# Values in front of a later duo's scores, in a bank of the first products, from block 1 on

## The chip, the cores and the metric

One core of a Trainium2 chip runs the whole program. The metric is the device time of one execution in microseconds (us). Below, PE is TensorE, PEld its weight loads, DVE VectorE, ACT ScalarE, POOL GpSimd and SP SyncE, whose queue issues the DMAs.

## The reference

```python
# q, k, v: (4, 8, 768, 64); mem_k, mem_v: 8 keys per head
for c in range(768 // 32):                      # chunks of 32 queries
    k_full = concat([mem_k, k[from 16 before the chunk to 8 behind it]])
    v_full = the same of mem_v, v
    s = q_c @ k_full.T / sqrt(64)
    a = exp(s - s.max(-1));  a = a / (a.sum(-1) + 1e-9)
    out[chunk] = a @ v_full
x = out, heads side by side                     # (3072, 512)
h = x @ w_in;  g = h * cos(h);  x = g @ w_out   # 512 -> 2048 -> 512
h = max(x @ w1, x @ w2, x @ w3);  x = h @ w_out2  # 512 -> 768 -> 512
```

The output is the last x, transposed, in fp32.

## The kernel before, in words

Each fp32 factor of the large products is split into a high and a low part, and a product is made as three passes over the parts (`PASSES`, `products`, L385 to L392). The program has two stages. The second, quads of the max of three products and the last product (`quad`, `pair_out`, lines L734 and L861), is not touched.

**The first stage** goes over `NBLK` = 6 blocks of 512 tokens, and within each over `FA` = 16 slots, one for each 128 of the 2048 columns of w_in. A slot (`slot`, from L980) issues:

- `p1`, the first products: 12 matmuls of 128x512 (L392, `h<-x,w`) into one bank, from the pool `ps_h` of two banks. The two banks are used in turn.
- `chain`: ACT rounds h (L450), DVE reduces it (L452, L453), ACT takes the sine (L455), DVE multiplies h with the cosine (L457), ACT takes the high part (L461) and POOL the low part (L462) of g. L457 is the last reader of the bank of h.
- `p2`, the second products of the slot two before (`LOOK` = 2): 12 matmuls (L392, `acc<-g`) into four accumulators. At a block's end they are copied out by ACT and DVE (L482, L484).

**Attention** for the following block is spread over these slots. A duo is 128 queries, four duos (`DB`) make a block, 24 (`ND`) the whole. The tables `FIRST` (block 0), `SECOND` (block 1) and `STEADY` (blocks 2 on) say what a slot does beside its products; a digit is a duo, counted from the next block's first, so 4 to 7 are duos of the block after next:

- S, scores: 32 small matmuls (L246) into two banks of the pool `ps_a`, two mask additions on DVE (L263), maximum and its subtraction (L269, L270), and the loads of q and k of two duos on.
- E, the exponentials of two duos on ACT (L274), with a table load ahead and another before the next sine.
- N, normalisation: sums (L279) and small operations on DVE, the product on POOL. T: a transpose on DVE and its store to DRAM. L or l: the load of the transposed weights `pt`.
- V, values: 32 small matmuls (L305) into a bank of `ps_a`, read by ACT (L307, the copy) and DVE (L308, the subtraction), which write the two parts of the next block's x.

What a slot's table names after T comes in the table's order. Before an S or a V the slot's second products were issued (`do2`), so PE ran first products, second products, attention. In block 4 nothing with a digit of 4 or more is left to do, and it is passed over. Preparation of the second stage's weights (L181, L198, L552, L553) runs on ACT, DVE and POOL beside the slots from slot 27 on. The orders of PE and SP are fixed as written from slot 6 on; ACT, DVE and POOL are ordered by the framework's scheduler, with parts of the chain held in line by `row`.

Of the kernel before, what the change touches and what calls it, by code (L numbers as in the profile page):

```python
# [9 lines left out]
F32 = mybir.dt.float32  # L10
# [13 lines left out]
S = 768  # L24
# [11 lines left out]
DB = N // (2 * QU)  # L36
# [11 lines left out]


FIRST = {2: "S0", 3: "S1", 4: "S2", 5: "S3 E01", 6: "E23 N0", 7: "T0 N1", 8: "L0 T1 N2", 9: "V0 l1", 10: "V1 T2 N3", 11: "L2 T3", 12: "V2 l3", 14: "V3"}  # L50
SECOND = {0: "S0", 1: "S1", 2: "E01 S2", 3: "N0 S3", 4: "T0", 5: "E23 N1 L0 S4", 6: "V0 T1", 7: "L1 N2", 8: "S5 T2 N3", 9: "V1 E45", 10: "L2 S6 T3", 11: "V2", 12: "L3 S7", 13: "V3", 14: "E67"}
STEADY = {1: "N0", 2: "T0 N1", 3: "L0", 4: "S4", 5: "V0 T1 N2", 6: "L1", 7: "S5", 8: "V1 T2 N3", 9: "L2 E45", 10: "S6 T3", 11: "V2 l3", 12: "S7", 13: "V3", 14: "E67"}

# [22 lines left out]
def attn_moe_kernel(ctx, tc, qT, kT, vw, w_in, w_out, w3, w2o, out):  # L78
# [23 lines left out]
    ps_h = ctx.enter_context(tc.tile_pool(name="ps_h", bufs=2, space=PSUM))  # L102
    ps_a = ctx.enter_context(tc.tile_pool(name="ps_a", bufs=2, space=PSUM))
# [145 lines left out]
    def a_scores(d):  # L249
        ss[d] = [ps_a.tile([128, 4, KU], F32, tag="a", name="s") for _ in range(2)]  # L250
        for t in range(2):
            a_s(d, t, ss[d][t], True, keep)
# [4 lines left out]
    def a_add(d):  # L257
        m = sm[d] = t2.tile([128, KB * H * 32], F32, tag="sm", name="sm", bufs=4)
        m = by_key(d)
        p = ss.pop(d)  # L260
        for t in range(2):
            mask = maskb[:, variant(d, t), None, :].to_broadcast([128, 4, KU])
            DVE.tensor_tensor(m[:, 4 * t:4 * t + 4], p[t].rearrange("p h (b k) -> p h b k", b=KB),  # L263
                              mask.rearrange("p h (b k) -> p h b k", b=KB), op=ALU.add)
# [7 lines left out]
    def a_exp(j, ds):  # L272
        for d in (DB * j + i for i in ds):
            keep(ACT.activation(out=sm[d], in_=sm[d], func=AF.Exp, scale=0.125))  # L274
# [14 lines left out]
    def a_l(d):  # L289
        pt[d] = t2.tile([128, 4, H, 32], F32, tag="pt", name="pt", bufs=1)  # L290
        for b in range(KB):
            keep(SP.dma_start(out=pt[d][32 * b:32 * b + 32].rearrange("p a h q -> p a (h q)"),
                              in_=ptd[d % 2][:, 256 * b:256 * b + 256].rearrange("(a p) e -> p a e", a=4)))

    def a_v(d):
        p, v = pt[d], vt[d]
        j, o = divmod(d, DB)
        if o == 0:
            xT[j] = xp.tile([128, 2, 4, N], F32R, tag="x", name="x")
        x = xT[j][:, :, :, 128 * o:128 * o + 128]  # L300
        s = ps_a.tile([128, 4, 128], F32, tag="a", name="s")
        for t in range(2):
            for h in range(H):
                p0 = 64 * (h % 2)
                keep(PE.matmul(s[p0:p0 + 64, h // 2, QU * t:QU * t + QU], lhsT=v[:KU, t, 64 * h:64 * h + 64],  # L305
                               rhs=p[:KU, 2 * (h % 2):2 * (h % 2) + 2, 4 * t + h // 2, :], start=True, stop=True))
        ACT.activation(out=x[:, 0], in_=s, func=AF.Copy)  # L307
        DVE.tensor_tensor(x[:, 1], s, x[:, 0].bitcast(F32), op=ALU.subtract)  # L308
# [85 lines left out]
    def p1(j, f):  # L394
        if f % 2 and (done[0] or j == 0 and f == 1):
            h = ps_a.tile([128, N], F32, tag="a", name="h")
        else:
            h = ps_h.tile([128, N], F32, tag="h", name="h")
        w, x = wA_in[f], xT[j]
        for k in range(4):  # L400
            products(h, w, k, [x[:, i, k, :] for i in range(2)], k == 0, k == 3)
        live[0] -= j == NBLK - 1
        hq[j, f] = h
# [4 lines left out]
    def wa_fetch(j, f):  # L408
        if j and f >= RES:
            w = w_tile([128, 2, 512], "wa")  # L410
            SP.dma_start(out=w.rearrange("p a c -> p (a c)").bitcast(F32), in_=wad[f])
            wA_out[f] = (w[:, 0, :], w[:, 1, :])
# [53 lines left out]
    def p2(j, f):  # L466
        g, w = g_t.pop((j, f)), wA_out[f]
        if f == 0:
            acc[j] = [ps_acc.tile([128, N], F32, tag=f"acc{m}", name=f"acc{m}") for m in range(4)]
        for m in range(4):  # L470
            products(acc[j][m], w, m, [g[:, i, :] for i in range(2 if j or f >= PLAIN else 1)], f == 0, f == FA - 1)
        live[0] -= f >= RES or j == NBLK - 1
        if f == FA - 1:
            for m in range(4):
                if m < 3:
                    t = tr.tile([128, N], F32, tag="r", name="x2")
                elif done[0]:
                    t = tmp["pool"].tile([128, N], F32, tag="xo", name="x2", bufs=6)
                else:
                    t = t2.tile([128, N], F32, tag="x2", name="x2", bufs=1)  # L480
                if m % 2 == 0:
                    ACT.activation(out=t, in_=acc[j][m], func=AF.Copy, scale=1.0 if j else -2.0)  # L482
                elif j:
                    DVE.tensor_copy(t, acc[j][m])  # L484
                else:
                    DVE.tensor_scalar(t, acc[j][m], -2.0, None, op0=ALU.mult)
                SP.dma_start(out=x2d[j][:, m, :], in_=t)
# [57 lines left out]
    def flush():  # L545
        while later:
            out, in_ = later.pop(0)
            keep(SP.dma_start(out=out, in_=in_))
# [61 lines left out]
    def prep_go(upto):  # L610
        while prep_n[0] < min(upto, len(prep)):
            prep[prep_n[0]]()
            prep_n[0] += 1
# [366 lines left out]
    def slot(s):  # L980
        j, f = slots[s]
        plan = {0: FIRST, 1: SECOND}.get(j, STEADY)
        todo = plan.get(f, "").split() if j < NBLK - 1 else []
        base = DB * (j + 1)

        ready = dec.nb
        if s < turn:
            dec.begin(RATE)
        if s < FA:
            parts = int(max(0, s - SPLIT0 + 1) * SPLITS[0])  # L990
        else:
            parts = int((FA - SPLIT0) * SPLITS[0] + (s - FA + 1) * SPLITS[1])

        def fill(where):
            if s < 2:
                if where == "z":
                    dec.split_in(ready)
                    dec.bits()
                    dec.load()
                return  # L1000
            if where == "z":
                prep_go(int(sum(i % FA not in QUIET for i in range(PREP0, s)) * PREPS))
            if s >= turn:
                if where == "z":
                    for fn in early.get(s - total, ()):
                        fn()
                return
            if where == "a0":
                dec.split_in(ready)
            elif where == "a1":  # L1010
                dec.split_out(parts)
            elif where == "d0":
                dec.bits(1)
            elif where == "z":
                dec.bits()
                dec.exp(dec.nb + 2)
                dec.load()

        for op in todo:
            if op[0] == "L" and base + int(op[1:]) < ND:  # L1020
                a_l(base + int(op[1:]))
        while wf[0] < min(s + (3 if s >= turn else 2), total):
            wa_fetch(*slots[wf[0]])
            wf[0] += 1
        flush()
        p1(j, f)
        chain(j, f, fill, [base + int(op[1:]) for op in todo if op[0] == "T" and base + int(op[1:]) < ND])

        def do2():
            while n2[0] <= s - LOOK:  # L1030
                p2(*slots[n2[0]])
                n2[0] += 1

        for op in todo:
            d = base + int(op[1:2])
            if d >= ND:
                continue
            if op[0] == "S":
                do2()
                a_scores(d)  # L1040
                a_add(d)
                a_load_qk(d + 2)
                a_max(d)
            elif op[0] == "E":
                a_exp(j + 1, map(int, op[1:]))
            elif op[0] == "N":
                a_norm(d)
            elif op[0] == "l":
                a_l(d)
            elif op[0] == "V":  # L1050
                do2()
                a_v(d)
                a_load_v(d + 2)
        do2()
# [32 lines left out]
    for p in range(NP):  # L1087
# [16 lines left out]
        todo = [["s11"], ["s1"], ["s3"], ["s21"], ["s2", "d4"], ["s22"], ["s4"]] if p + 1 < NP else []  # L1104
# [67 lines left out]
```

## Time and profile before

| | |
|---|---|
| median of three runs | 967.79 us (967.32 to 967.80) |
| profiled execution | 966.72 us |
| its span | 964.6 us |
| PE busy | 955.1 us, 99% of the span |
| DVE, ACT, POOL busy | 616.5, 461.4 and 410.3 us |

The profile shows one execution. The span runs from the first to the last recorded work; the execution's own time is 2.1 us longer. A busy engine's share is over both stages.

### The profile page before, as it was taken

How to read it: one execution, taken by the hardware profiler on the slowest of the kernel's cores; microseconds unless marked ns; L12 is line 12 of the kernel's file. 1: busy time of each engine (PE TensorE's matmuls, PEld its weight loads, DVE VectorE, ACT ScalarE, POOL GpSimd, SP SyncE). 2: the span in 40 equal slices, each digit the busy share in tenths (PEclk: the TensorE clock that was granted, in tenths of full speed). 3: DMA queues.
4: the chain of work that ended last, by engine and by line, in shares of the span. 5: the costliest groups of instructions: out<-in, count | busy, mean ns of one | idle time of the engine just before them, and what ended most of it. 6: DMA issues, size and time to landing. Idle time of an engine off the chain costs nothing.

```text
span 964.6 us, 14585 instructions
## 1 busy us (share of the span) xinstructions
PE 955.1 (99%) x5372; PEld 770.3 (80%) x5373; DVE 616.5 (64%) x926; ACT 461.4 (48%) x802; POOL 410.3 (43%) x329
## 2 busy tenths in 40 slices
PE   8999999999999999999999999999999999999998
PEld 5666888888888888888888888888888888888886
DVE  7688856655667666665655475644784657945565
ACT  6667745555445554564544545523363332723333
POOL 3566535534345445445433355435511545025520
PEclk9999999999999999999999999999999999999999
DMA  9986633563556855675476739694569647595502
GB/s 291 341 300 198 224 128 105 162 197 141 188 198 227 245 196 181 211 237 181 152 243 226 235 113 325 225 319 164 175 229 325 247 137 227 200 390 174 198 22 88
DMA packets 75911, 201.75 MB, mean 209 GB/s; under 512 B 8256, under 2 KB 21056, under 8 KB 75840
## 3 DMA queue, kind: packets, MB, share of 16 engines
q1 hardware_dynamic: 75552, 200.56, 61.9%
q8 instruction: 43, 0.70, 0.3%
q10 hardware_dynamic: 288, 0.26, 0.1%
q14 instruction: 28, 0.23, 0.1%
HBM read 154.13 MB, written 46.66 MB: 208 GB/s over the span
## 4 chain that ended last, share of the span: by engine, by line
PE 94%; DVE 3%; ACT 1%; issue 1%; DMA 1%; POOL 0%; SPq 0%; DVEq 0%; ACTq 0%
PE hb L734 27%; PE h L392 26%; PE acc L392 23%; PE hb L861 9%; PE s L246 3%; PE acc L389 3%; PE s L305 2%; PE warm L375 1%; DMA pt<-ptd 1%; PE s L356 0%; ACT ki L455 0%; DVE ki L453 0%; DVE ki L452 0%; DVE ki L457 0%; DVE mx L322 0%
## 5 line engine op out<-in xcount | busy, mean ns | idle before, releaser
L392 PE MATMUL h<-x,w 128*128 128x512 f32 x1152 | 283.8, 396 | 0.0
L392 PEld LDWEIGHTS h<-x,w 128*128 128x128 f32 x1152 | 213.2, 188 | 48.6 <-issue 1.4
L462 POOL TENSOR_TENSOR g<-ki,g 128x512 fp32r<-128x512 f32 x80 | 108.6, 1357 | 213.0 <-ACT g L461 186.9
L734 PE MATMUL hb<-x,wq 128*128 128x512 f32 x648 | 155.7, 389 | 0.0
L734 PEld LDWEIGHTS hb<-x,wq 128*128 128x128 f32 x648 | 121.6, 188 | 25.2
L392 PE MATMUL acc<-g,w 128*128 128x512 f32 x576 | 138.3, 389 | 0.0
L392 PEld LDWEIGHTS acc<-g,w 128*128 128x128 f32 x576 | 108.2, 188 | 22.4
L734 PE MATMUL hb<-xo,wq 128*128 128x512 f32 x486 | 119.1, 389 | 0.0
L392 PE MATMUL acc<-g,wa 128*128 128x512 f32 x480 | 115.6, 389 | 0.2 <-POOL g L462 0.2
L455 ACT ACTIVATE ki<-ki,pio 128x512 f32<-128x512 f32 x80 | 57.9, 723 | 109.3 <-DVE ki L453 109.3
L734 PEld LDWEIGHTS hb<-xo,wq 128*128 128x128 f32 x486 | 91.2, 188 | 18.9
L392 PEld LDWEIGHTS acc<-g,wa 128*128 128x128 f32 x480 | 90.0, 188 | 19.3 <-POOL g L462 0.6
L760 POOL TENSOR_TENSOR p<-p,p 128x512 f32<-128x512 f32 x27 | 38.3, 1420 | 144.9 <-ACT p L757 144.9
L452 DVE SCALAR_TENSOR_TENSOR ki<-h,ki 128x512 f32<-128x512 f32 x80 | 54.9, 687 | 69.3 <-ACT ki L450 69.3
L457 DVE TENSOR_TENSOR ki<-h,ki 128x512 f32<-128x512 f32 x80 | 55.2, 690 | 54.9 <-ACT ki L455 54.9
L861 PE MATMUL hb<-g,wo 128*128 128x512 f32 x378 | 86.2, 389 | 0.0
L861 PEld LDWEIGHTS hb<-g,wo 128*128 128x128 f32 x378 | 71.0, 188 | 14.7
L461 ACT ACTIVATE g<-ki 128x512 fp32r<-128x512 f32 x80 | 50.5, 631 | 59.3 <-DVE ki L457 59.1
L450 ACT ACTIVATE ki<-h 128x512 int32<-128x512 f32 x80 | 47.2, 590 | 60.0 <-PE h L392 53.5
L760 DVE TENSOR_TENSOR a<-a,hb 128x512 f32<-128x512 f32 x27 | 18.5, 684 | 72.1 <-PE hb L734 72.1
L553 DVE TENSOR_TENSOR wq<-raw,wq 128x512 fp32r<-128x512 f32 x36 | 44.1, 1243 | 25.0 <-ACT wq L552 25.0
L198 DVE SCALAR_TENSOR_TENSOR raw<-raw,top 128x512 int32<-128x512 int32 x48 | 46.1, 960 | 13.1 <-ACT top L181 11.7
(127 smaller groups left out, 1212.3 us busy)
## 6 DMA issues: line engine op xcount, KB each, us to landing
wq<-wd SPq DMA_DIRECT2D x81, 512.0 KB, 6.6
wa<-wad SPq DMA_DIRECT2D x40, 512.0 KB, 5.9
wo<-wod SPq DMA_DIRECT2D x30, 512.0 KB, 4.3
wd<-wq SPq DMA_DIRECT2D x27, 512.0 KB, 2.7
v<-in_vw_dram SPq DMA_DIRECT2D x24, 384.0 KB, 6.3
raw<-in_w_dram SPq DMA_DIRECT2D x18, 511.8 KB, 5.5
raw<-in_w_in_dram SPq DMA_DIRECT2D x16, 511.8 KB, 10.3
raw<-in_w_out_dram SPq DMA_DIRECT2D x16, 511.8 KB, 10.1
```

The lines of the kernel that those rows point to most:

```text
L198: keep(DVE.scalar_tensor_tensor(o, z, 13, top[key], op0=ALU.logical_shift_right, op1=ALU.bitwise_or))
L392: PE.matmul(o, lhsT=w[a][:, sl], rhs=x[b], start=first and n == 0, stop=last and n == 2)
L450: row(ACT.activation(out=ki, in_=h, func=AF.Copy, scale=INV2PI, bias=0.25))
L452: row(DVE.scalar_tensor_tensor(c, h, INV2PI, ki, op0=ALU.mult, op1=ALU.subtract))
L455: row(ACT.activation(out=c, in_=c, func=AF.Sin, scale=2 * math.pi, bias=pio2))
L457: row(DVE.tensor_tensor(c, h, c, op=ALU.mult))
L461: row(ACT.activation(out=g[:, 0, :], in_=c, func=AF.Copy))
L462: row(POOL.tensor_tensor(g[:, 1, :], c, g[:, 0, :].bitcast(F32), op=ALU.subtract))
L553: keep(eng.tensor_tensor(w[:, 1, :], src, w[:, 0, :].bitcast(F32), op=ALU.subtract))
L734: keep(PE.matmul(o, lhsT=w[:, a, 256 * half + 128 * c:256 * half + 128 * c + 128], rhs=x[c][:, b, :], start=first and n == 0, stop=n == 5, ...
L760: keep(eng.tensor_tensor(o, a, b, op=op))
L861: keep(PE.matmul(bk[i][b], lhsT=w[:, s, x, 128 * i:128 * i + 128], rhs=g[:, y, :], start=b not in seen and c == 0 and m == 0, stop=c == 2 ...
```

## The change

The tables put a scores step into the slot of a values step: in blocks 2 on "V0 S4" in slot 5, "V1 S5" in 8, "V2 S6" in 11 and "V3 S7" in 13; in block 1 in slots 6, 8, 11 and 13. The exponentials of duos 4 and 5 go from slot 9 to slot 10, of 6 and 7 from slot 14 to slot 15. Where a slot's table has both, the second products are no longer issued ahead of them, so PE runs first products, values, scores, second products. From the ninth duo on (`d >= 2 * DB`, values computed in block 1 or later) the values' bank is taken from `ps_h` instead of `ps_a`.

```diff
-SECOND = {0: "S0", 1: "S1", 2: "E01 S2", 3: "N0 S3", 4: "T0", 5: "E23 N1 L0 S4", 6: "V0 T1", 7: "L1 N2", 8: "S5 T2 N3", 9: "V1 E45", 10: "L2 S6 T3", 11: "V2", 12: "L3 S7", 13: "V3", 14: "E67"}
-STEADY = {1: "N0", 2: "T0 N1", 3: "L0", 4: "S4", 5: "V0 T1 N2", 6: "L1", 7: "S5", 8: "V1 T2 N3", 9: "L2 E45", 10: "S6 T3", 11: "V2 l3", 12: "S7", 13: "V3", 14: "E67"}
+SECOND = {0: "S0", 1: "S1", 2: "E01 S2", 3: "N0 S3", 4: "T0", 5: "E23 N1 L0", 6: "V0 S4 T1", 7: "L1 N2", 8: "V1 S5 T2 N3", 10: "L2 E45 T3", 11: "V2 S6", 12: "L3", 13: "V3 S7", 15: "E67"}
+STEADY = {1: "N0", 2: "T0 N1", 3: "L0", 5: "V0 S4 T1 N2", 6: "L1", 8: "V1 S5 T2 N3", 9: "L2", 10: "E45 T3", 11: "V2 S6 l3", 13: "V3 S7", 15: "E67"}
...
-        s = ps_a.tile([128, 4, 128], F32, tag="a", name="s")
+        late = d >= 2 * DB
+        s = (ps_h if late else ps_a).tile([128, 4, 128], F32, tag="h" if late else "a", name="s")
...
             if op[0] == "S":
-                do2()
+                if not any(o[0] == "V" for o in todo):
+                    do2()
...
             elif op[0] == "V":
-                do2()
+                if not any(o[0] == "S" for o in todo):
+                    do2()
```

On PE, block 2 across slots 4 and 5 (`h` first products, `acc` second products, L246 scores, L305 or L306 values), before:

```order
L246 MATMUL s_2655<-k_2157,q_2156 64x96 x8
L246 MATMUL s_2656<-k_2157,q_2156 64x96 x8
L392 MATMUL h_2683<-x_1893,w_746 128x512 x12
L392 MATMUL acc0_2564<-g_2603,w_1619 128x512 x3
L392 MATMUL acc1_2565<-g_2603,w_1619 128x512 x3
L392 MATMUL acc2_2566<-g_2603,w_1619 128x512 x3
L392 MATMUL acc3_2567<-g_2603,w_1619 128x512 x3
L305 MATMUL s_2726<-pt_2580,v_2218 64x64 x16
L392 MATMUL h_2757<-x_1893,w_809 128x512 x12
```

The same place in the changed program, whose lines count one more from here on:

```order
L393 MATMUL h_2655<-x_1853,w_746 128x512 x12
L306 MATMUL s_2686<-pt_2580,v_2178 64x64 x16
L246 MATMUL s_2707<-k_2202,q_2201 64x96 x8
L246 MATMUL s_2708<-k_2202,q_2201 64x96 x8
L393 MATMUL acc0_2564<-g_2603,w_1619 128x512 x3
L393 MATMUL acc1_2565<-g_2603,w_1619 128x512 x3
L393 MATMUL acc2_2566<-g_2603,w_1619 128x512 x3
L393 MATMUL acc3_2567<-g_2603,w_1619 128x512 x3
L393 MATMUL h_2757<-x_1853,w_809 128x512 x12
```

Two separate pieces of attention, each between a second and a first product, became one piece between a first and a second product.

On PE, block 4 across slots 5 and 6, where no scores are left, before:

```order
L392 MATMUL h_4456<-x_3626,w_746 128x512 x12
L392 MATMUL acc0_4365<-g_4404,w_1619 128x512 x3
L392 MATMUL acc1_4366<-g_4404,w_1619 128x512 x3
L392 MATMUL acc2_4367<-g_4404,w_1619 128x512 x3
L392 MATMUL acc3_4368<-g_4404,w_1619 128x512 x3
L305 MATMUL s_4496<-pt_4381,v_4018 64x64 x16
L392 MATMUL h_4526<-x_3626,w_809 128x512 x12
```

The same place in the changed program:

```order
L393 MATMUL h_4456<-x_3586,w_746 128x512 x12
L306 MATMUL s_4484<-pt_4381,v_3982 64x64 x16
L393 MATMUL acc0_4365<-g_4404,w_1619 128x512 x3
L393 MATMUL acc1_4366<-g_4404,w_1619 128x512 x3
L393 MATMUL acc2_4367<-g_4404,w_1619 128x512 x3
L393 MATMUL acc3_4368<-g_4404,w_1619 128x512 x3
L393 MATMUL h_4526<-x_3586,w_809 128x512 x12
```

The values alone moved in front of the second products, and the rest stands as it did.

On DVE, block 2, slot 10, before, the slot of the scores of duo 6 (L279 sums, L263 mask additions, L269 the maximum, L452, L453 and L457 the chain's three operations on one h):

```order
L279 TENSOR_REDUCE rs_3411<-sm_2673 128x8
L279 TENSOR_REDUCE rs_3464<-sm_2861 128x8
L452 SCALAR_TENSOR_TENSOR ki_2997<-h_2984,ki_2997 128x512
L280 TENSOR_SCALAR rs_3411<-rs_3411 128x8
L263 TENSOR_TENSOR sm_3044<-s_3026,maskb_91 128x4x3x32
L453 TENSOR_SCALAR ki_2997<-ki_2997 128x512
L263 TENSOR_TENSOR sm_3044<-s_3027,maskb_91 128x4x3x32
L281 RECIPROCAL rs_3411<-rs_3411 128x8
L269 TENSOR_REDUCE mx_3051<-sm_3044 128x8
L280 TENSOR_SCALAR rs_3464<-rs_3464 128x8
L281 RECIPROCAL rs_3464<-rs_3464 128x8
L457 TENSOR_TENSOR ki_2997<-h_2984,ki_2997 128x512
```

The same in the changed program, slot 11, where those scores and the third values now are (L309 the subtraction that empties the values' bank, L453, L454 and L458 the chain):

```order
L279 TENSOR_REDUCE rs_3411<-sm_2725 128x8
L263 TENSOR_TENSOR sm_3097<-s_3079,maskb_91 128x4x3x32
L453 SCALAR_TENSOR_TENSOR ki_3042<-h_3029,ki_3042 128x512
L309 TENSOR_TENSOR x_2685<-s_3058,x_2685 128x4x128
L454 TENSOR_SCALAR ki_3042<-ki_3042 128x512
L263 TENSOR_TENSOR sm_3097<-s_3080,maskb_91 128x4x3x32
L280 TENSOR_SCALAR rs_3411<-rs_3411 128x8
L279 TENSOR_REDUCE rs_3464<-sm_2910 128x8
L269 TENSOR_REDUCE mx_3104<-sm_3097 128x8
L458 TENSOR_TENSOR ki_3042<-h_3029,ki_3042 128x512
```

The values' subtraction, which had a slot of its own before, now stands with the mask additions and the sums among the three operations of one chain.

## Rows read from the trace of the kernel before

**Rows 1.** The page's head, busy times, and weight loads (busy us, mean ns).
```profile
span 964.6 us, 14585 instructions
PE 955.1 (99%) x5372; PEld 770.3 (80%) x5373; DVE 616.5 (64%) x926; ACT 461.4 (48%) x802; POOL 410.3 (43%) x329
L392 PEld LDWEIGHTS h<-x,w 128*128 128x128 f32 x1152 | 213.2, 188 | 48.6 <-issue 1.4
```

**Rows 2.** What PE waited for: us in total, times, longest.
```profile
PE s L305 <- DMA pt<-ptd: 0.8, 1, 0.8
```

**Rows 3.** Timeline of PE, block 2: start us, duration, engine, line, operation, number of instructions.
```profile
294.93 2.88 PE L392 MATMUL h<-x,w 128*128 128x512 f32 x12
297.65 2.88 PE L392 MATMUL acc<-g,wa 128*128 128x512 f32 x12
300.46 1.54 PE L246 MATMUL s<-k,q 64*64 64x96 f32 x32
301.93 3.06 PE L392 MATMUL h<-x,w 128*128 128x512 f32 x12
304.82 2.88 PE L392 MATMUL acc<-g,wa 128*128 128x512 f32 x12
307.63 1.15 PE L305 MATMUL s<-pt,v 96*64 96x64 f32 x32
311.57 2.88 PE L392 MATMUL acc<-g,wa 128*128 128x512 f32 x12
```

**Rows 4.** The same, cut inside each piece; then each line's shortest, median, longest matmul (ns).
```profile
300.84 1.16 PE L246 MATMUL s<-k,q 64*64 64x96 f32 x24
307.86 0.93 PE L305 MATMUL s<-pt,v 96*64 96x64 f32 x26
L246 PE MATMUL s<-k,q x768: 242/243/419, 6.1 to 414.9; 64*64 64x96 f32 x192
L305 PE MATMUL s<-pt,v x640: 221/222/272, 89.7 to 513.9; 96*64 96x64 f32 x160
```

**Rows 5.** Timeline, all engines, block 4, slot 5 and the start of slot 6.
```profile
460.05 2.88 PE L392 MATMUL h<-x,w 128*128 128x512 f32 x12
...
466.47 0.69 DVE L457 TENSOR_TENSOR ki<-h,ki 128x512 f32<-128x512 f32 x1 [0.79 <-ACT ki L455]
466.66 3.02 PE L392 MATMUL h<-x,w 128*128 128x512 f32 x12
```

**Rows 6.** Timeline, all engines, block 4, slots 8 and 10.
```profile
477.67 2.88 PE L392 MATMUL h<-x,w 128*128 128x512 f32 x12
...
482.96 1.00 DVE L453 TENSOR_SCALAR ki<-ki 128x512 f32<-128x512 f32 x1
...
489.86 2.88 PE L392 MATMUL h<-x,w 128*128 128x512 f32 x12
...
497.68 0.69 DVE L457 TENSOR_TENSOR ki<-h,ki 128x512 f32<-128x512 f32 x1 [0.79 <-ACT ki L455]
```

**Rows 7.** Timeline, all engines, block 1, slot 5 and the chain of slot 6.
```profile
162.45 2.88 PE L392 MATMUL h<-x,w 128*128 128x512 f32 x12
...
168.90 1.22 DVE L263 TENSOR_TENSOR sm<-s,maskb 128x384 f32<-128x384 f32 x2 [0.27 <-PE s L246]
...
170.67 1.58 ACT L274 ACTIVATE sm<-sm 128x768 f32<-128x768 f32 x2
...
175.23 0.69 DVE L457 TENSOR_TENSOR ki<-h,ki 128x512 f32<-128x512 f32 x1 [0.61 <-ACT ki L455]
```

**Rows 8.** Timeline, ACT, block 2, slot 9: the table load ahead of two exponentials.
```profile
297.05 1.28 ACT L274 ACT_TABLE_LOAD   x1
```

**Rows 9.** Timeline, all engines, block 3, slot 1, with the copy of an accumulator of block 2.
```profile
339.09 2.88 PE L392 MATMUL h<-x,w 128*128 128x512 f32 x12
...
346.45 0.68 DVE L484 COPY x<-acc 128x512 f32<-128x512 f32 x1
...
348.25 0.69 DVE L457 TENSOR_TENSOR ki<-h,ki 128x512 f32<-128x512 f32 x1 [0.19 <-ACT ki L455]
```

## The prediction

> **What bounds the kernel now.** The page's head and busy times come first: PE works 955.1 of 964.6 us [rows 1], so only what shortens or interrupts PE's stream changes the end. The table of waits says how far others hold PE up: in the part that the change touches it names one wait of 0.8 us for a load [rows 2]. What can be gained lies inside the stream, so the timeline of PE comes next, in one stretch of block 2, and after it the timelines of all engines at the places where the new order takes time away from DVE and ACT.
>
> In block 2 [rows 3] first products start at 294.93 and second products 2.72 later, at 297.65, so a slot without attention is 5.44. From those second products to the next, with scores between, it is 304.82 - 297.65 = 7.17: a scores step costs 1.73. From there on, with values, 311.57 - 304.82 = 6.75: a values step costs 1.31.
>
> How much of it is the change between kinds of work is read by cutting the pieces [rows 3, 4]. All 32 scores matmuls span 1.54, the last 24 of them 1.16. A record ends about 0.24 after it starts, so 24 records are 23 steps in 1.16 - 0.24, or 0.040 each, and 32 stream in 1.28. That leaves 0.45 for getting in and out. For values 26 records last 0.93, one 0.22: 0.71 over 25 steps is 0.0284, 32 stream in 0.91, and 0.40 is left. Getting in is the small part: scores start 0.09 behind the end of the second products (300.46 against 297.65 + 2.72), and the first eight run 0.38 against 0.32, together 0.15; getting out is the other 0.30.
>
> **The change, part by part.**
>
> *Merging.* Values and scores of one slot now follow each other on PE. There are 12 such pairs, four in each of blocks 1, 2 and 3. Work stays equal; one way in and one way out vanish, and a direct change from values to scores comes instead. The trace of before has none. What vanishes is about 0.40 (the smaller overhead). If the direct change is free, that is the gain: 12 x 0.40 = 4.8. If it costs a whole way out and in, the gain is 0. I take it as a way in, 0.15, the nearest row, since both pieces are small matmuls whose weights load in the same way. Gain 0.25 per pair, **-3.0** in all; a merged slot should then last 5.44 + 1.73 + 1.31 - 0.25 = 8.23.
>
> The Trainium skill, "TensorEngine Tiling (Array Packing)", section "Key Properties", says that changing the tiling mode drains TensorE, and not just changing the tile. Values take 96x64 weights and scores 64x64, so the direct change would be one of these drains too: a pair goes from four to three, and with all four alike (a quarter of 0.85, an estimate) the gain would be 0.21 per pair, 2.5 in all. No row here shows such a change yet.
>
> *The values' bank.* It comes from the first products' pool now. With three users in a merged slot's neighbourhood for two banks, PE gets a condition that it did not have: in the built order the first products behind a merged slot mostly take the bank that the values have just used and wait for the subtraction that empties it, and those one slot later wait for the h cos h product of the merged slot. Call e the end of a slot's first products in the records. The next first products start at e + 8.23 - 2.88 = e + 5.35, and their weights load 0.19 earlier [rows 1]: whatever frees the bank by e + 5.16 costs nothing. In block 4 no scores are left, values stand alone between first and second products, and the limit is shorter: 466.66 - 462.93 = 3.73 less 0.19, or e + 3.54 [rows 5]. The places, each with what is late:
>
> - Block 4, slot 5: the first products of slot 6 take the bank of slot 5's own h. Its last reader, L457, ends at 467.16 [rows 5], e + 4.23. That is 0.69 late; behind PE, all of it is on the path. **+0.7** (bounds 0.3 and 1.3).
> - Block 4, slot 8: the subtraction stands behind L453, which ends at 483.96, e + 3.41 with e = 480.55 [rows 6]; as long as L457 (0.69), it ends at e + 4.10. Late by 0.56, but that L453 took over twice its usual time beside POOL. **+0.3** (0 to 0.6).
> - Block 4, slot 11: the values take the bank of slot 10's h, freed at 498.37, or e + 5.63 with e = 492.74 [rows 6]. Values start at e + 5.37, one slot of 5.44 less the modelled end. **+0.3** (0 to 0.7).
> - Block 1, slot 6: with the scores gone from slot 5, slot 6's first products end 1.73 earlier against the exponentials of duos 2 and 3. Those end at 172.25 [rows 7], 6.92 behind e of slot 5 (165.33), so e + 1.48 for slot 6. Before, L457 of that slot ended at 175.92, 3.67 behind them. The same delay gives e + 5.15 against 5.16, and up to two mask additions, 1.22 together, now stand in between. **+0.3** (0 to 1.2).
> - Values 2.72 earlier elsewhere: their loads have to be there. In blocks 2 on the starts now lead by 2.72, and the load waited for before [rows 2] is in block 0, which keeps its order. I put **+0.2** (0 to 1) on this and on slot 13, where values wait for slot 12's h.
>
> Together +1.8. In slots 8, 11 and 13 of blocks 2 and 3 I take the limit as kept: DVE, 64% busy [rows 1], has the values' subtraction behind one chain operation there.
>
> *Exponentials one slot later.* Two of them and a table load, 1.28 + 1.58 = 2.86 of ACT [rows 7, 8], move from slot 9 to 10 and 14 to 15. Nothing is added, but the second batch now reaches the block's end, where accumulators are copied. In slot 1 of block 3, L457 ends at 348.94, e + 6.97 with e = 341.97, and the copy of the second accumulator at 347.13, e + 5.16 [rows 9]. Needed are e + 7.8 (slot 3's first products take that bank, two slots of 5.44 on, less 2.88 and 0.19) and about e + 5.7 (the second group of the next block's first second products). So 0.8 and 0.6 are free. I cost it at nothing; if this cover fails, PE stands in the first slots of blocks 2, 3 and 4.
>
> *Sum.* 966.72 - 3.0 + 1.8 = 965.5 in the profiled execution. The median lies 1.07 above that execution, so **966.6**.
>
> **The rivals.**
>
> - *All gain.* The waits do not come, since the scheduler's order and the trace's lateness at four single places are coincidences of this run: -3.0. Or the direct change is free and the waits come: -4.8 + 1.8 = -3.0. For it: all waits worked out are under 1 us. Against: the block 4 wait follows from one row. Median 964.8, with both together 963.0.
> - *Slower: the exponentials land on the accumulator copies.* Place: slot 1 of blocks 2, 3 and 4. It decides from a lateness of 0.6 to 0.8 beyond before. ACT is busy 48% [rows 1], so a slot gives it 2.8 to catch up, and a batch one slot later can put its work up to 2.8 later: 2.0 beyond the limit, at worst. At 1.4 each, three ends cost 4.2: -3.0 + 1.8 + 4.2 = +3.0, median 970.8. For it: the margin is under a third of what is moved. Against: the sine that follows needs its own table load in either slot, and the scheduler can put the copies first.
> - *The change does not do what it says:* values to scores costs a full way out and in, and the merged slots last 8.5, not 8.2. Gain 0, waits remain: +1.8, median 969.6. For it: two different tile shapes. Against: getting in was the small part.
>
> **How the numbers follow.** A measurement of this kernel tells 0.2%, about 1.9 us, from no change: faster is below 965.9, slower above 969.7. The forecast, gain partly given back, spans 965.1 (all waits at their low ends, 0.3 together) to 968.1 (halfway to their high ends, 3.3) and has 0.50; a third of it lies below 965.9. All gain has 0.27, most of it faster. The exponentials have 0.14, nearly all slower; the dear change 0.09, half slower. Faster 0.38, same 0.43, slower 0.19. The range takes in most of the cases beside: 964.4 to 970.3, with half of "both together" and the dearer half of the exponentials left out, 2 in 10.
>
> **What would show it.** Merged slots, from second products to second products, last 8.2 (right), 8.5 (nothing gained) or 8.1 (a free change). The table of waits has first products behind DVE's L458 or L309 in block 4, slots 6, 9 and 11, each under 1 us. In slot 1 of blocks 2 to 4, L458 ends before e + 7.8 and no second products wait for a copy. I am wrong if PE waits at the block ends, if a merged slot in blocks 2 or 3 is followed by a wait, or if values wait for their load.

## The result and the profile after

The changed kernel takes **974.82 us** (median of six runs, 970.53 to 975.87), the kernel before 967.20 (966.52 to 967.80): a ratio on record of 1.0069, 95% interval 1.0054 to 1.0084 (the two medians alone give 1.0079). By the medians it is 7.6 us slower; 966.6 was forecast, with 964.4 to 970.3 as the range.

The page's head, busy times and chain of the changed kernel, against [rows 1]; the last line is the chain of before:

```profile
span 973.2 us, 14598 instructions
PE 953.6 (98%) x5373; PEld 771.8 (79%) x5373; DVE 622.0 (64%) x926; ACT 462.4 (48%) x802; POOL 410.6 (42%) x329
PE 77%; DVE 10%; ACT 5%; DMA 3%; issue 3%; SPq 0%; POOL 0%; DVEq 0%; ACTq 0%; POOLq 0%
...
PE 94%; DVE 3%; ACT 1%; issue 1%; DMA 1%; POOL 0%; SPq 0%; DVEq 0%; ACTq 0%
```

PE is busy for 1.5 us less than before in a span 8.6 us longer. The time went into gaps, and the chain that ended last (the work that set the end, followed back) now spends 18% of the span in DVE, ACT and DMA, where it was 5%. The table of PE's waits (us in total, times, longest) names them, against [rows 2]:

```profile
PE s L306 <- DVE ki L458: 6.2, 3, 2.7
PE s L306 <- DMA pt<-ptd: 2.6, 2, 1.8
PE h L393 <- DVE ki L458: 1.1, 1, 1.1
```

Three times values wait for a chain's last reading of h, L458 (L457 before), once first products do, and a values step waits for its load (the second wait of that line is in block 0, as before). The timeline of the changed kernel's PE shows where (columns as in [rows 3]; in brackets the idle time before and what ended it):

```profile
186.47 1.15 PE L306 MATMUL s<-pt,v 96*64 96x64 f32 x32 [1.78 <-DMA pt<-ptd]
...
319.34 1.15 PE L306 MATMUL s<-pt,v 96*64 96x64 f32 x32 [1.83 <-DVE ki L458]
...
420.32 1.45 PE L306 MATMUL s<-pt,v 96*64 96x64 f32 x32 [2.67 <-DVE ki L458]
...
473.45 3.01 PE L393 MATMUL h<-x,w 128*128 128x512 f32 x12 [1.06 <-DVE ki L458]
...
506.71 1.15 PE L306 MATMUL s<-pt,v 96*64 96x64 f32 x32 [1.75 <-DVE ki L458]
```

These are block 1, slot 8; slot 13 of blocks 2 and 3; and block 4, slots 6 and 11. Where nothing waits, a pair looks like this, in slot 11 of block 2:

```profile
300.97 2.88 PE L393 MATMUL h<-x,w 128*128 128x512 f32 x12
303.78 1.15 PE L306 MATMUL s<-pt,v 96*64 96x64 f32 x32
304.87 1.54 PE L246 MATMUL s<-k,q 64*64 64x96 f32 x32
306.33 3.02 PE L393 MATMUL acc<-g,wa 128*128 128x512 f32 x12
309.19 2.88 PE L393 MATMUL h<-x,w 128*128 128x512 f32 x12
```

From first products to first products it is 309.19 - 300.97 = 8.22, and 13.66 with a plain slot of 5.44. Before, two slots with both steps took 311.57 - 297.65 = 13.92 [rows 3]. A pair gains **0.26**.

The next timeline shows, in block 3, how slot 13's values came to stand (PE, the chains' last readings, and what lay ahead of them on ACT and DVE):

```profile
405.30 1.58 ACT L274 ACTIVATE sm<-sm 128x768 f32<-128x768 f32 x2
...
406.78 0.58 ACT L451 ACTIVATE ki<-h 128x512 int32<-128x512 f32 x1
...
409.32 2.88 PE L393 MATMUL h<-x,w 128*128 128x512 f32 x12
...
410.43 0.94 DVE L269 TENSOR_REDUCE mx<-sm 128x8 f32<-128x768 f32 x1
411.29 0.68 DVE L458 TENSOR_TENSOR ki<-h,ki 128x512 f32<-128x512 f32 x1
...
413.23 3.37 DVE L554 TENSOR_TENSOR wq<-raw,wq 128x512 fp32r<-128x512 f32 x2
...
414.76 2.88 PE L393 MATMUL h<-x,w 128*128 128x512 f32 x12
...
417.24 1.55 DVE L454 TENSOR_SCALAR ki<-ki 128x512 f32<-128x512 f32 x1
418.82 0.72 ACT L456 ACTIVATE ki<-ki,pio 128x512 f32<-128x512 f32 x1 [4.58 <-DVE ki L454]
419.57 0.69 DVE L458 TENSOR_TENSOR ki<-h,ki 128x512 f32<-128x512 f32 x1 [0.79 <-ACT ki L456]
```

The exponentials, now in slot 10, hold slot 11's rounding (L451) back to 406.78, where its first products end at 403.99. DVE puts sums, mask additions, the values' subtraction and the maximum into the same chain, which ends at 411.97. Then two pieces of weight preparation (L554) keep DVE for 3.37, and slot 12's chain, whose first products ended at 412.20, frees its bank at 420.26, 8.06 behind them. Slot 13's values took that bank; the limit was 5.37.

The wait has a second price. Busy times of the engines in short stretches of block 3 behind it (stretch, its length, then PE, PEld, DVE, ACT, POOL, the granted clock, DMA share and GB/s):

```profile
420.00:422.00 2.00, 1.68 (x36) 1.56 (x38) 0.49 (x2) 1.63 (x4) 1.00 (x1) 0.75 0.00 0
422.00:424.00 2.00, 2.00 (x29) 2.00 (x27) 1.81 (x3) 1.12 (x2) 0.97 (x2) 0.50 0.04 8
424.00:426.00 2.00, 2.00 (x15) 1.52 (x12) 1.93 (x4) 0.64 (x2) 0.53 (x1) 0.90 0.91 289
426.00:428.00 2.00, 2.00 (x10) 1.64 (x9) 1.18 (x2) 0.80 (x1) 2.00 (x2) 1.00 1.01 307
```

After PE had stood for 2.67 us, its clock fell to the lower of its two levels, 1.2 GHz, until some 424, and the scores took 2.83 instead of 1.54. In block 2 the wait of 1.83 left the clock alone in this execution. Of the six runs, one had a granted clock of 1.000 over its span and took 970.53; the other five had 0.996 to 0.998 and took 974.25 to 975.87. In the profiled execution (0.998) this fall is 1.7 of the 8.4 us. Two falls, as in e1 below with its 0.996, cost 3.3; four of the five other runs have 0.996 too, so an estimate for them is 3.3 of 7.6. What else made the run at 1.000 shorter is not shown.

### The profile page after: what moved, and what is told of

It reads as the page before. It is cut to its first block, busy times and chain, and to the rows that moved or that the text cites. A ratio compares the mean times of both kernels' runs of the same rounds, so it can differ in the third digit from the quotient of the medians.

```text
span 973.2 us, 14598 instructions
## 1 busy us (share of the span) xinstructions
PE 953.6 (98%) x5373; PEld 771.8 (79%) x5373; DVE 622.0 (64%) x926; ACT 462.4 (48%) x802; POOL 410.6 (42%) x329
## 4 chain that ended last, share of the span: by engine, by line
PE 77%; DVE 10%; ACT 5%; DMA 3%; issue 3%; SPq 0%; POOL 0%; DVEq 0%; ACTq 0%; POOLq 0%
PE hb L735 26%; PE h L393 18%; PE acc L393 16%; PE hb L862 9%; PE acc L390 3%; PE s L246 3%; DVE ki L458 2%; DVE ki L453 2%; ACT ki L456 2%; PE s L306 2%; DVE ki L454 1%; DMA raw<-in_w_dram 1%; DVE wq L554 1%; DMA pt<-ptd 1%; ACT wq L553 1%
## 5 line engine op out<-in xcount | busy, mean ns | idle before, releaser
L393 PE MATMUL h<-x,w 128*128 128x512 f32 x1152 | 279.9, 392 | 1.1 <-DVE ki L458 1.1
L453 DVE SCALAR_TENSOR_TENSOR ki<-h,ki 128x512 f32<-128x512 f32 x80 | 54.9, 687 | 86.6 <-ACT ki L451 84.4
L458 DVE TENSOR_TENSOR ki<-h,ki 128x512 f32<-128x512 f32 x80 | 55.1, 689 | 50.8 <-ACT ki L456 50.8
L451 ACT ACTIVATE ki<-h 128x512 int32<-128x512 f32 x80 | 47.0, 588 | 63.3 <-PE h L393 56.9
L554 DVE TENSOR_TENSOR wq<-raw,wq 128x512 fp32r<-128x512 f32 x36 | 46.8, 1322 | 21.7 <-ACT wq L553 21.6
```

The source lines that it names most:

```text
L393: PE.matmul(o, lhsT=w[a][:, sl], rhs=x[b], start=first and n == 0, stop=last and n == 2)
L451: row(ACT.activation(out=ki, in_=h, func=AF.Copy, scale=INV2PI, bias=0.25))
L453: row(DVE.scalar_tensor_tensor(c, h, INV2PI, ki, op0=ALU.mult, op1=ALU.subtract))
L458: row(DVE.tensor_tensor(c, h, c, op=ALU.mult))
L554: keep(eng.tensor_tensor(w[:, 1, :], src, w[:, 0, :].bitcast(F32), op=ALU.subtract))
```

## The experiments

Theory A: PE waits because values in front of the second products need, 2.7 us earlier than before, a bank that a chain still reads, or their load. Rival B: the later exponentials are the harm by themselves. Rival C: most of the loss is the clock behind one wait. Rival D: DVE's work, piled up in a merged slot, is the cause wherever the banks are.

The stretch before block 1, which no run changes, lasts from 127.35 to 132.25 us in the profiled executions, so the runs are also compared by the lengths of their blocks in the profiled execution. A block runs here from slot 0's first products to those of the next block's slot 0 (us):

```
run                                  block 1  block 2  block 3  block 4
before                                106.13    99.20    99.20    92.27
changed                               107.14   100.13   102.56    95.51
e1  block 4 in the old bank           107.15   102.03   102.46    92.26
e2  exponentials in slot 9            106.41    98.93    99.47    94.02
e3  last pair in slot 14              106.50    99.19    99.56    93.71
e4  exponentials later, alone         106.13    99.29    99.20    92.26
e5  old bank everywhere               116.62   104.30   106.78    92.27
e6  second products first             107.73    98.63    98.39    94.86
e7  four places mended                105.28    98.75    99.63    92.26
e8  e7, pairs a slot later            105.28   104.33   102.24    92.27
e9  bank alone                        106.14   103.15   103.29    93.94
e10 e7, second first from block 2     105.29    98.34    98.29    92.27
e11 e10, exponentials in slot 10      105.29    98.26    98.31    92.27
e12 e7, second first in slot 11       105.29    99.60   100.15    92.26
```

The changed kernel's blocks are 1.01, 0.93, 3.36 and 3.24 longer than before, 8.5 together, where the two profiled executions differ by 8.4 (975.10 against 966.72); block 5 and all that follows are equal.

**e1, block 4 in the old bank.**

```diff
-        late = d >= 2 * DB
+        late = 2 * DB <= d < ND - DB
```

> Only the four values steps of block 4 take their bank from the old pool again; their place in front of the second products stays. Theory A (PE waits for a bank that the chain of the slot before still reads): the two waits of block 4 go, 1.4 us in front of slot 6's first products and 1.9 us in front of slot 11's values, so about 3.4 less than the changed kernel's 974.8, near 971.4; slots 5, 8, 11 and 13 of block 4 then all step 3.87 us from the end of first products to the next. Rival B (the later exponentials are the harm, whatever bank is used): block 4 has no exponentials, its waits are left over from block 3, and the time stays within 1 us of 974.8. Rival C (most of the loss is TensorE's clock behind the wait of slot 13 in block 3): also within 1 us, since that wait stays.

Measured 972.32 (ratio 1.0053, 1.0039 to 1.0066); block 4 lasts 92.26 as before, 3.25 less than changed. Block 4's whole loss goes with the bank; the order, values in front of the second products, stays and costs nothing. B falls for block 4. C falls as well: it held the time within 1 us of 974.8 as long as slot 13 of block 3 waits, which it does here, and 2.5 went. Slot 13 still waits, and this time the clock fell behind the wait in block 2 too:

```profile
318.89 1.83 PE L306 MATMUL s<-pt,v 96*64 96x64 f32 x32 [1.83 <-DVE ki L458]
320.66 2.41 PE L246 MATMUL s<-k,q 64*64 64x96 f32 x32
```

The same wait of 1.83 as in the changed kernel, and block 2 is 1.9 longer than there.

**e2, exponentials of duos 4 and 5 in slot 9.**

```diff
-STEADY: ... 9: "L2", 10: "E45 T3"
+STEADY: ... 9: "L2 E45", 10: "T3"
-SECOND: ... 10: "L2 E45 T3"
+SECOND: ... 9: "E45", 10: "L2 T3"
```

> The changed kernel with the exponentials of duos 4 and 5 back in slot 9, the rest as changed. Theory A: the bank's condition only moves: slot 10's chain is late as before the change (it ended 7.7 us behind its first products), so the values in slot 11 wait some 2.3 us for it in blocks 2 and 3, while slot 12's chain is early again and slot 13 does not wait. Sum: minus 6.2 (1.9 in block 2, 4.3 in block 3 with its slow clock) plus 4.6: 973 to 975. Rival B: the later slot was the harm and nothing takes its place: 974.8 - 6.2 = 968.6, no wait in slot 11 or 13.

Measured 969.08 (1.0026, 1.0016 to 1.0036), nearly B's number, but not by B's way, which had no wait in slot 11. Slot 13 no longer waits for a chain, as A said, but slot 11 waits 0.40 and 1.22, not 2.3: slot 10's chain ended 5.8 and 6.6 behind its first products, not 7.7; the scores that had shared slot 10 before are in slot 11 now, which fits, though no run varies it alone. In blocks 2 and 3 the slot of the exponentials is worth 4.3 us to the changed kernel, the slow clock included. Another 1.5 went in block 4, which this edit does not touch: its slot 11 does not wait here, nor in e3. The section on the prediction shows why.

**e3, last pair in slot 14.**

```diff
-STEADY: ... 13: "V3 S7", 15: "E67"
+STEADY: ... 14: "V3 S7", 15: "E67"
```

> In blocks 2 and later the last values and the scores that follow them go from slot 13 to slot 14. Theory A: they then wait for slot 13's chain, which has a slot more to catch up (slot 12's ended 7.2 to 8.1 us behind its first products, slot 13's should end by about 5), so the waits of 1.8 and 2.7 us in blocks 2 and 3 go, and with them the half clock behind the second: 974.8 - 6.2 = 968.6, granted clock 1.000. In block 4 the lone values move a slot, nothing else. Rival B: the lateness comes from the exponentials and stays as a wait in slot 14 or in the next block's first slots: over 972.

Measured 970.49 (1.0035, 1.0022 to 1.0049). The waits shrink to 0.89 and 1.31, since slot 13's chains still ended 6.3 and 6.7 behind, and four of six runs kept a clock of 1.000. A holds in kind, not in size, and 1.8 of the gain is block 4's slot 11 again; the lateness takes more than a slot to work off.

**e4, exponentials later, alone.**

```diff
-STEADY (before): ... 9: "L2 E45", 10: "S6 T3", ... 14: "E67"
+STEADY:          ... 9: "L2", 10: "S6 E45 T3", ... 15: "E67"
```

`SECOND` alike.

> The kernel before with one part of the change alone: the exponentials of duos 4 and 5 in slot 10 and of 6 and 7 in slot 15. Values and scores keep their slots, order and banks. Theory A: nothing waits for the chains of slots 11 and 12 there, so within 0.2% of the kernel before, 966 to 969. Rival B: chains come late and PE stands at the block's end or behind slot 11: 4 to 7 us slower than before, 971 to 974.

Measured 966.82, ratio 0.9996 (0.9985 to 1.0007), and every block as before. The later exponentials cost nothing where nobody waits for the chains behind them: B alone falls.

**e5, old bank everywhere.**

```diff
-        late = d >= 2 * DB
+        late = False
```

> The changed kernel with every values step in a bank of the old pool again; merged slots, order and exponentials as changed. Theory A (the bank decides where PE waits): no values wait for a chain any more (minus 1.8 and 2.7 us in slot 13, and its slow clock), and block 4 loses its two waits, but the scores behind the values need two banks of a pool of two, of which the values hold one, so their second half waits for the subtraction that empties it: the values' bank took about 2.1 us from the end of the values to the end of the subtraction, the first half of the scores covers 0.65, so 1 to 2 us in each of 12 pairs. About 974.8 - 9.6 + 18 = 983 (977 to 992). Rival D (the merged place itself piles up DVE and the bank does not matter): no new wait of the scores, 966 to 971.

Measured 993.75 (1.0277, 1.0249 to 1.0306), beyond A's range (977 to 992). PE's waits in its profile:

```profile
PE s L246 <- DVE x L309: 16.4, 9, 3.9
PE s L246 <- DVE sm L263: 4.3, 3, 2.4
```

All 12 pairs wait for the values' bank or for one that a mask addition empties, 1.7 us on average, within A's 1 to 2; the clock, which A's sum left out, was 0.987 to 0.997. So the merged place needs another bank, as the change has it; D falls.

**e6, second products first.**

```diff
             elif op[0] == "V":
-                if not any(o[0] == "S" for o in todo):
-                    do2()
+                do2()
```

> The changed kernel with the second products issued ahead of a values step again, so PE runs first products, second products, values, scores. Theory A: values start 2.7 us later, so the load in block 1 (1.8) and the chains of slot 12 (1.8 and 2.7 late) are there in time, and the slow clock goes; but the first products that follow the scores take the bank that the values used and had 2.8 us more for before: they wait 0.3 to 1.5 us behind most of the 12 pairs for the subtraction or a chain, and behind the lone values of block 4 too (1.4 in slot 5). About 974.8 - 8.1 + 8 = 975 (969 to 982). Rival D (it is the pile of work on DVE in a merged slot, wherever PE has it): the same pile is there, with waits of the same size moved to the first products, 974 to 977 and waits in slots 11 to 13 alone.

Measured 970.07 (1.0026, 1.0013 to 1.0040), in A's range but 5 below its number: A had waits behind most of the 12 pairs. Slot 13's waits are gone. The first products behind the scores wait 1.26 in two slots of block 1 and hardly at all in blocks 2 and 3; block 4 keeps 2.6. The pair gains the same in this order.

**e7, four places mended.** Block 4's bank and order as before, the second pair of block 1 a slot later, e2's slot in `STEADY`.

```diff
+        todo = [op for op in todo if base + int(op[1]) < ND]
...
+        late = 2 * DB <= d < ND - DB
...
+SECOND: ... 8: "T2 N3", 9: "V1 S5", 10: "L2 E45 T3"
+STEADY: ... 9: "L2 E45", 10: "T3"
```

> The change with its four places mended: exponentials of duos 4 and 5 in slot 9 from block 2 on, the pair of slot 8 in block 1 in slot 9, and block 4's values behind the second products in the old pool. Theory A: left are the waits of 0.4, 0.2 and 1.2 us that the run with slot 9 alone showed in blocks 2 and 3; the load in block 1 (1.0 to 1.8), block 4's 1.7 and the 0.14 of each lone place go. Merging gives 12 x 0.26 = 3.1. Against the kernel before: -3.1 + 1.8 = -1.3, 965.6 where before is 966.9, clock 1.000. Rival D or B: stays at 968 to 971, since DVE's pile is still there.

Measured 967.30, ratio 0.9997 (0.9988 to 1.0007): no difference, where 1.3 was expected. The blocks shorten by 0.9 in the profiled execution. Block 1 gains 0.9, and has no wait left; in blocks 2 and 3 slot 11's two waits, 0.40 and 1.39, take back what merging gives there.

**e8, pairs a slot later.** e7, and:

```diff
-STEADY: ... 11: "V2 S6 l3", 13: "V3 S7"
+STEADY: ... 12: "V2 S6 l3", 14: "V3 S7"
```

> As the run with all waits avoided, and from block 2 on the third and fourth pair in slots 12 and 14 instead of 11 and 13. Theory A: slot 11's chain is a slot further from the exponentials of slot 9 and ends under 5.4 us behind its first products, so no values wait at all: -3.1 against the kernel before, 963.8 where before is 966.9. It is wrong if the fourth pair, so close to slot 15's exponentials, holds up the next block's first slots: then 966 or more, with waits in slots 1 to 3.

Measured 978.75 (1.0113, 1.0096 to 1.0130): a miss. Block 3 lost 1.17 to slot 11's chain, which A had in time, but the load was the larger matter. SP's issues in block 2 (start, duration):

```profile
313.87 3.58 SPq L169 DMA_DIRECT2D raw<-in_w_dram  x2
...
318.92 1.38 SPq L292 DMA_DIRECT2D pt<-ptd  x3
```

The load of the last values, moved with the third pair, now stands behind two weight loads, 3.58 together, and the values waited 4.36 for it (2.73 in block 3).

**e9, bank alone.** The change's bank in the kernel before, nothing else.

```diff
-        s = ps_a.tile([128, 4, 128], F32, tag="a", name="s")
+        late = d >= 2 * DB
+        s = (ps_h if late else ps_a).tile([128, 4, 128], F32, tag="h" if late else "a", name="s")
```

> The kernel before with one part of the change alone: from block 1 on the values' bank comes from the first products' pool. Order, slots and exponentials as before. Theory A: values, 2.7 us later than in the changed kernel, find their bank free, but the first products right behind them take the bank of the slot's own chain, whose end is allowed 3.54 us behind the first products' end. In the trace of before it was later in seven of the sixteen slots with values: 6.0 and 6.6 in slot 11 of blocks 2 and 3, 4.0 and 4.1 in their slots 13, 4.2, 4.9 and 4.4 in block 4; the sum over the limit is 9.4 us. So 976 (972 to 980), with waits of 2.5 and 3.1 us in slot 11. Rival D (DVE's pile in merged slots is the cause, not the bank): nothing is merged here, so within 0.2% of before.

Measured 977.00 (1.0111, 1.0097 to 1.0124): A's 976, with waits where it put the largest. That the number fits is in part luck. Of the 9.7 us that blocks 2 to 4 grew, 6.5 are waits, where A had 9.4 with two in slots 13 that did not come; 3.2 are the slow clock, which A had not counted.

```profile
310.74 4.60 PE L393 MATMUL h<-x,w 128*128 128x512 f32 x12 [2.27 <-DVE ki L458]
...
414.04 4.60 PE L393 MATMUL h<-x,w 128*128 128x512 f32 x12 [2.41 <-DVE ki L458]
```

Here the first products behind the wait ran at the lower clock, 4.60 for what takes 3.02 behind values at the full one. Nothing is merged and no exponentials move: the bank by itself costs 10 us.

**e10, second products first from block 2 on.** e7, and:

```diff
-                if not any(o[0] == "S" for o in todo):
+                if j > 1 or not any(o[0] == "S" for o in todo):
                     do2()
```

> As the run with all waits avoided, and from block 2 on the second products go ahead of the pair (first products, second products, values, scores). Theory A: values of slots 11 then start 2.7 us later, 8.1 us behind the end of the slot before's first products, and its chain (5.8 and 6.8 us in that run) is done; the 0.46 and 1.46 us go. The first products behind the scores find the bank late by 0.2 us at most, as the run with second products first showed in blocks 2 and 3. Block 1 shortens by 0.9, blocks 2 and 3 by 0.9 each: 2.7 less than the kernel before, clock 1.000. Rival D: as much as there, no difference to before.

Measured **964.45** (963.60 to 965.58), ratio 0.9980, 0.9971 to 0.9988: faster than both kernels. Block 3, slot 11, as it should be:

```profile
399.57 2.88 PE L393 MATMUL acc<-g,wa 128*128 128x512 f32 x12
...
402.38 1.15 PE L306 MATMUL s<-pt,v 96*64 96x64 f32 x32
403.46 1.54 PE L246 MATMUL s<-k,q 64*64 64x96 f32 x32
...
405.07 3.01 PE L393 MATMUL h<-x,w 128*128 128x512 f32 x12
```

PE's table and timeline show no wait in blocks 1 to 4. DVE has the same work in the merged slots as in e7, so D, which had no gain here, falls by this run too.

**e11, the same with exponentials in slot 10.**

```diff
-STEADY: ... 9: "L2 E45", 10: "T3"
+STEADY: ... 9: "L2", 10: "E45 T3"
```

> As the run with second products ahead of the pair from block 2 on, but with the exponentials of duos 4 and 5 in slot 10. Theory A: with the pair that late the exponentials' slot no longer matters much: blocks 2 and 3 as in the run with second products first everywhere (0.6 and 0.8 shorter than before), 2.2 less than before in all. Rival B: the waits of slot 13 come back, blocks 2 and 3 a microsecond or more longer than before.

Measured 964.45, ratio 0.9980 (0.9971 to 0.9989). A holds: with values 2.7 us later the exponentials' slot, worth 4.3 us in the change's order, is worth nothing.

**e12, second products first in slot 11 alone.** e7, and:

```diff
+                if j > 1 and f == 11 or not any(o[0] == "S" for o in todo):
                     do2()
```

> As the run with all waits avoided, with second products ahead of the pair in slot 11 of blocks 2 on alone. Theory A: the waits of 0.46 and 1.46 us in slot 11 go, the rest stays as it was there: block 1 shorter by 0.9, blocks 2 and 3 by 1.0 each, 2.9 less than the kernel before. It is wrong if slot 13's values, whose order is as changed, wait for slot 12's chain, which the later scores of slot 11 push back by a part of a microsecond.

Measured 965.65, ratio 0.9990 (0.9981 to 0.9999), 1.2 less than before where 2.9 was expected. Slot 11's waits went, but in the profiled execution, the slowest of its runs, slot 13's values waited 1.63 for slot 12's chain in block 3, as the expectation named for its failing, and 1.15 for their load in block 2, which it did not name.

## Why the prediction was wrong

**The merging** was right: 0.25 a pair forecast, 0.26 measured where nothing waits, 3.1 in all. The prediction's other price, by its estimate with a quarter for each of four changes, was 0.21. The measured 0.26 lies nearer to 0.25, but either share was assumed. The Trainium skill, "TensorEngine Tiling (Array Packing)", section "Key Properties", says that changing the tiling mode drains TensorE. No run here shows whether the direct change does.

**The waits** were the error: +1.8 forecast, 11.4 measured (a slot's length over what it takes with no wait); the blocks' 8.5 are -3.1 + 11.4 and 0.2 in small delays. Step by step:

- Block 4, slot 5: 0.7 forecast, 1.42 measured. The chain ended 5.11 behind its first products, not 4.23 as before, because the rounding started 0.9 later against PE. Those 0.9 are the later exponentials' work. In e4, where nothing else is changed, slot 5's chain of block 4 ends at 467.62, 5.13 behind its first products, and in e9, with the exponentials as before, 4.22 behind. The batch of slot 15 makes slot 0's chain 0.9 later, and five slots do not catch it up. The prediction looked at slot 1 alone and carried 4.23 over from before:

```profile
459.61 2.88 PE L392 MATMUL h<-x,w 128*128 128x512 f32 x12
...
464.27 0.56 ACT L450 ACTIVATE ki<-h 128x512 int32<-128x512 f32 x1
...
466.93 0.69 DVE L457 TENSOR_TENSOR ki<-h,ki 128x512 f32<-128x512 f32 x1 [0.79 <-ACT ki L455]
```

- Block 4, slot 8: 0.3 forecast, none. Slot 11: 0.3 forecast, 1.81. Slot 10's chain ended at e + 7.1, not e + 5.63. Its rounding stood on ACT behind a weight's unpacking (L181), which waited for that weight's load:

```profile
496.64 2.88 PE L393 MATMUL h<-x,w 128*128 128x512 f32 x12
...
502.55 0.79 ACT L181 ACTIVATE top<-raw 128x512 f16<-128x512 bf16 x1 [1.95 <-DMA raw<-in_w_dram]
503.20 0.57 ACT L451 ACTIVATE ki<-h 128x512 int32<-128x512 f32 x1
```

The load of that weight set the 5.63 of before as well (L181 waited 2.09 there), and over the runs the chain's end at this place goes from e + 3.8 (e6) to e + 7.1. So the row told when a load came in one execution, as the rival "all gain" suspected of single places.

- Block 1, slot 6: 0.3 forecast, 0.05. The delay behind the exponentials came out as worked out (L458 at e + 5.33).
- "I put +0.2 on this and on slot 13, where values wait for slot 12's h" is the step that failed. The load in block 1 cost 1.84, slot 13 in block 2 1.91, in block 3 4.34 with its slow clock: **8.1**, where +0.2 stood.

Why block 1's load was late: the prediction counted values 2.72 earlier, but `SECOND` also moves V1 from slot 9 to slot 8. Before, these values started at 194.51 with their load issued from 180.25 on; in the changed kernel the load is issued from 180.46 on, and PE would have started the values at 186.47 - 1.78 = 184.69, some 9.8 earlier. With that pair in slot 9, e7 has no wait there.

Why slot 13 went wrong can be read from before. There, in block 3, slot 12's chain ran as follows:

```profile
407.91 3.02 PE L392 MATMUL h<-x,w 128*128 128x512 f32 x12
...
415.57 0.69 DVE L457 TENSOR_TENSOR ki<-h,ki 128x512 f32<-128x512 f32 x1 [0.19 <-ACT ki L455]
```

It ended at 416.26, 5.33 behind the end of its first products at 410.93, with 5.37 as the limit: 0.04 to spare (0.66 in block 2, where the wait was the smaller), with the exponentials' sums and the third scores in slot 10. The change puts both into slot 11, one slot nearer, and the prediction did not ask how late slot 12 becomes. "In slots 8, 11 and 13 of blocks 2 and 3 I take the limit as kept" looked only at the bank of the first products behind a pair, which was indeed free; the values' own bank was the one that bound. DVE's 64% was no argument for one stretch: from 410 to 416 DVE was busy for 5.93 of 6.00 us.

**The exponentials** were costed at nothing, with the block ends as the rival. The block ends held: in slot 1 of blocks 2 and 3 the chain ended at e + 7.55, limit 7.8, and no copy was waited for. Alone the shift costs nothing (e4). But in the change's order it makes slot 13's wait (e2) and the larger part of block 4's first one, places that the slower rival did not name. That rival had the sign and the exponentials, and not the mechanism.

**The clock** had no term. A granted clock of 1.000 over the whole of before was taken for granted. One fall is 1.7 of the 8.4 us in the profiled execution, and by the estimate above two are 3.3 of 7.6 in the runs at 0.996.

So three parts of the change act together. The bank lets a pair exist (e5), and makes PE depend on the chain's end (e9). Values ahead of the second products shorten that limit by 2.7 us (e6, e10), and the exponentials, DVE's work for the pair and two pieces of preparation make the chain late just there. The exponentials' part is shown (e2); that of DVE's work for the pair and of the preparation is read from the trace, and no run takes either away. With the order taken back from block 2 on and block 1's and block 4's places mended, no wait is left even with the exponentials in slot 10 (e11), and the merging's gain remains: 2.4 us.

## What to carry to other kernels

Before a step is given a buffer that another chain also uses, list for every place the end of that chain's last reader against the step's new start, also in the slots next to the ones that the change speaks of: a margin of 0.04 us lasts only until something moves nearer. Ask too what set that end. A chain that stood behind a load in one execution ends elsewhere in the next. A step's order inside its slot can be worth more than the slot: here 2.7 us of delay for the values cleared what two other moves only lessened. And where PE has had no gaps, price a new gap with the clock behind it, here 1.6 to 1.7 us each time that it fell.

## What was not expected of the hardware

Gaps on PE of nearly equal length did not always cost the clock. Behind 1.83 us in slot 13 of block 2 the granted clock stayed at 1.00 in the changed kernel and fell to 0.50 in e1, at the same place; behind 2.67 and 2.44 in block 3 it fell in both, and behind 2.73 in e8 it stayed at 1.00. Where it fell, the slot lost 1.6 to 1.7 us more (the changed kernel, e1 and e9). The Trainium skill, "TensorE: Matmul & The Clock Gate", section "Part 1: The HAM clock gate (the "warmup" mystery)", says that the clock's gate goes by how busy PE has been lately. The rows agree in kind: every fall in blocks 1 to 4 stands behind a gap. They also show that the same code behind the same gap pays in one execution and not in another. Second, L454, which in block 3 took 0.41 in slot 11, took 1.55 in slot 12 with POOL at work beside it, and L554 3.37 for two pieces, of 1.32 each on the page's mean: how long a chain's DVE part lasts is not fixed.
